# Stack loads in SyncE's queue, stores a cycle later, and maxima split before their transpose, in a fused attention and Fourier-mixing kernel

## Chip, cores and metric

One Trainium2 chip, one of its cores. The metric is the device time of one execution in microseconds (us), as the median over several runs. A second figure, the span, comes from one profiled execution and goes from its first to its last instruction.

## The reference

Two blocks read the same `x` of 2048 rows by 640 columns, and a gate mixes them row by row. All is float32.

```python
def _A_ref(x, wqkv, wo):                 # attention: H = 32 heads of Dh = 20
    qkv = (x @ wqkv).reshape(B, S, 3, H, Dh)   # then q, k, v by head
    scores = einsum("bhqd,bhkd->bhqk", q, k) * Dh ** -0.5
    p = softmax(scores, axis=-1)
    o = einsum("bhqk,bhkd->bhqd", p, v)
    return o.reshape(B, S, D) @ wo
def _B_ref(x, seq_re, seq_im, hid_re, hid_im):   # real part of a 2-D DFT
    a = einsum("bsd,ed->bse", x, hid_re)
    b = einsum("bsd,ed->bse", x, hid_im)
    return einsum("ts,bse->bte", seq_re, a) - einsum("ts,bse->bte", seq_im, b)
g = sigmoid((x * gate_w).sum(-1, keepdims=True))
return g * _A_ref(x, wqkv, wo) + (1 - g) * _B_ref(x, ...)
```

## The kernel before

Products that need more than one pass of TensorE's rounded float32 are written as three products of a value split into a rounded part and a remainder (`split`, `three`). q, k and v are projected first; q and k go in two parts to `qk_scr` in device memory, v to `v_scr`.

Attention works by units: 32 units, each of two heads and half of the 2048 queries; two units that share their heads are a pair. For a pair, `load_stack` brings k's parts into one of two `kst` buffers and q's parts into one of two `qst` buffers by 12 DMAs (four for k, four for each half of the queries): 40 rows from both parts at once, and 20 rows from the first part. A unit has 32 steps. Each step `e` computes, for two heads, a 128x512 block of transposed scores (L685) and its exponential on ScalarE (L687). The maximum that the softmax subtracts is computed ahead by a second pass over the scores (`m`, L159) and a reduction on VectorE (L161); this pass runs LEAD = 41 steps ahead. When a unit's maxima are complete, `max_nm` reduces them to 128x16 with the sign turned, `max_chain` transposes that on TensorE (L193), splits the result into `m1` and `m2`, and four DMAs write the rows into `qst`, where they act as two more rows of the contraction. `av_step` (L448) multiplies probabilities with v and a column of ones, which gives the sum of each row.

After a unit, `unit_end` copies the accumulator to `o` (ScalarE) and lists its follow-ups by steps: store the row sums (`store_l`), load them spread over partitions (`load_l`), reciprocal on VectorE (`recip`), store and broadcast it (`store_r`, `load_r`), multiply `o` on GpSimd (`norm`) and store it (`store_o`).

The Fourier block fills TensorE's room in the same loop. `hid_tile` makes the hidden-dimension products (stored to `a_scr`), and from about 640 us on `dft_step` does the sequence dimension in 56 units of 16 steps: `load_c` brings DFT matrices (`in_cdft`), `load_a` the operand (`araw`), both added and split on GpSimd; results are summed over several units through `y_scr` (`yt` is an earlier sum loaded again, `finish_y` adds and stores).

The order is written out by hand. One cycle is four steps of attention, and the string gives the order of TensorE's instructions in it: `e` and `m` one score matmul each, `F` a share of the fill, `B` the burst of 16 `av` matmuls, with the maxima's reduction ahead of them and their transpose behind. All DMAs and off-path work are listed with `at_step(i, fn)` and issued when step `i` begins:

```python
ORDER = "emFemFFFFemFeFFmeFFemFFFmmFFmeeB"
def burst(c):
    for n in ends:
        max_nm(n)
    run_extras(max(done - HIDS, 0) // 3, 2)
    for kt in (2 * c, 2 * c + 1):
        av_step(now[0], kt // NS, kt % NS)
    while ends:
        max_chain(ends.pop(0))
```

SyncE (SP) carries nearly all DMAs in one queue, in the order of the steps; an instruction that waits holds those behind it. GpSimd (POOL) carries the stack's DMAs among its additions and splits. At the end, `rest` holds the follow-ups of the last unit, and the output product runs tile by tile.

Of the kernel before, what the change touches and what calls it, by code (L numbers as in the profile page):

```python
# [10 lines left out]
F32 = mybir.dt.float32  # L11
R = mybir.dt.float32r
AF = mybir.ActivationFunctionType
ALU = mybir.AluOpType
AX = mybir.AxisListType
# [3 lines left out]
P = 128  # L19
# [7 lines left out]
HE = D // 2  # L27
VW = 2 * (DH + 1)
KROWS = 3 * DH
NU = 2 * NP  # L30
# [25 lines left out]
UNITS = len(PRODUCTS) * HT  # L56


def f32(ap):
    return ap.bitcast(F32)  # L60
# [3 lines left out]
def mix_kernel(ctx: ExitStack, tc: tile.TileContext, xa, wqk, wb, cdft, wo, out):  # L64
# [8 lines left out]
    small = pools(name="small", bufs=1)  # L73
# [24 lines left out]
    def split(dst1, dst2, src, e1, e2):  # L98
        if e1 is act:
            act.activation(dst1, src, AF.Copy)  # L100
        else:
            e1.tensor_copy(dst1, src)  # L102
        e2.tensor_tensor(dst2, src, f32(dst1), op=ALU.subtract)  # L103
# [8 lines left out]
    def bank():  # L112
        return ps_w.tile([P, 512], F32, name=f"ps{next(turn) % 5}")
# [13 lines left out]
    def load_stack(p):  # L127
        kt, qt = kst[p % 2], qst[p % 2]
        u = S // 2
        for t, o, two, one, cs in ((kt, D, 0, 2, slice(0, S)), (qt, 0, 1, 0, slice(0, u)), (qt, 0, 1, 0, slice(u, S))):  # L130
            for h in range(2):
                r = (2 * p + h) * DH
                b = 64 * h
                rows = slice(o + r, o + r + DH)
                yield f32(t[b + two * DH : b + (two + 2) * DH, cs]), qk_scr[:, rows, cs]
                yield f32(t[b + one * DH : b + (one + 1) * DH, cs]), qk_scr[0, rows, cs]
# [8 lines left out]
    def at_step(i, fn):  # L145
        later.setdefault(i, []).append(fn)
# [24 lines left out]
            max_chain(n - 1)  # L171

    def max_nm(n):
        nms[n] = small.tile([P, 16], F32, name="nm", bufs=2)
        dve.tensor_reduce(nms[n], mx.pop(n).rearrange("p h q c -> p (h q) c"), axis=AX.X, op=ALU.max, negate=True)

    def s_step(i):
        for fn in [s_mm(i, h) for h in range(2)]:
# [10 lines left out]

    def max_chain(n):  # L190
        q = q_unit(n)
        pt = bank()[:16, :P]
        pe.transpose(pt, nms.pop(n), ident)  # L193
        m1 = small.tile([16, P], R, name="m1", bufs=2)
        m2 = small.tile([16, P], R, name="m2", bufs=2)
        split(m1, m2, pt, dve, dve)

        def rows():
            for h in range(2):
                b = 64 * h + KROWS  # L200
                sp.dma_start(f32(q[b : b + 1, :]), f32(m1[8 * h : 8 * h + 8, :]))
                sp.dma_start(f32(q[b + 1 : b + 2, :]), f32(m2[8 * h : 8 * h + 8, :]))

        if now[0] < 0:
            rows()
        else:
            at_step(now[0] + 2, rows)


    pa = pools(name="att", bufs=1)  # L210
# [195 lines left out]
    def load_c(g):  # L406
        n, j = divmod(g, 2)
        n, t = divmod(n, HT)
        raws = []
        for i, (_, th, ri) in enumerate(PRODUCTS[n][0]):  # L410
            raw = apool[0].tile([P, 1024], F32, name="raw2", bufs=2) if i and apool else raw_tile()
            o = (2 * ri + j) * 1024
            sp.dma_start(raw, cdft[th * HT + t, :, o : o + 1024])
            raws.append(raw)

        def finish():
            c = cparts[g] = part_tile()
            if len(raws) > 1:
                pool.tensor_tensor(raws[0], raws[0], raws[1], op=ALU.add if PRODUCTS[n][0][1][0] > 0 else ALU.subtract)  # L419
            split(c[:, 0], c[:, 1], raws[0], pool, pool)  # L420

        return finish
# [28 lines left out]
            unit_end(i, n)  # L451

    def unit_end(i, n):
        o = pa.tile([P, 512], F32, name="o")
        act.activation(o, av, AF.Copy)
        lc = pa.tile([P, 16], F32, name="lc")
        rb = pa.tile([P, 512], F32, name="rb")

        q = pool if n == NU - 1 else sp

        def store_l():
            q.dma_start(l_scr[n], o.rearrange("(j r) c -> j r c", j=4)[:, DH])

        def load_l():
            q.dma_start(lc, l_scr[n].rearrange("j (a b) -> (j a) b", b=16))

        def recip():
            dve.reciprocal(lc, lc)

        def store_r():  # L470
            q.dma_start(r_scr[n].rearrange("j (a b) -> (j a) b", b=16), lc)

        def load_r():
            for j in range(4):
                q.dma_start(rb[32 * j : 32 * j + 32, :], r_scr[n, j : j + 1].to_broadcast([32, 512]))

        def norm():
            pool.tensor_tensor(o, o, rb, op=ALU.mult)  # L478

        def store_o():  # L480
            for qc in range(2):
                for h in range(2):
                    j = 2 * qc + h
                    t0 = (n % 2) * (S // 2) + qc * 512
                    r = (2 * (n // 2) + h) * DH
                    q.dma_start(o_scr[r : r + DH, t0 : t0 + 512], o[32 * j : 32 * j + DH, :])

        steps = (1, 4, 10, 12, 15, 23, 25) if n < NU - 2 else (1, 4, 10, 12, 15, 19, 21)
        for k, fn in zip(steps, (store_l, load_l, recip, store_r, load_r, norm, store_o)):
            if n == NU - 1:  # L490
                rest.append(fn)
            else:
                at_step(i + k, fn)
# [7 lines left out]
    def dft_step(g):  # L501
        n, t, s = g // NS // HT, g // NS % HT, g % NS
        if s == 0:
            new_y(0), new_y(1)
            outs[n, t] = []
            for _, th, hf in PRODUCTS[n][2]:
                tt = th * HT + t
                y = None
                if (tt, hf) in signs:
                    y = apool[0].tile([P, HE], F32, name="yt", bufs=4)  # L510
                    sp.dma_start(y, y_scr[tt, :, hf * HE : (hf + 1) * HE])
                outs[n, t].append(y)
        if s % 8 == 0 and g // 8 + 3 < 2 * UNITS:
            cfin.append(load_c(g // 8 + 3))
        if s % 8 == 4 and cfin and g // 8 + 2 < 2 * UNITS:
            cfin.pop(0)()
        c = cparts[g // 8]
        cs = slice((s % 8) * P, (s % 8 + 1) * P)
        a = at[n % 2, s]
        for z, (cz, az) in enumerate(((0, 0), (0, 1), (1, 0))):  # L520
            for h in range(2):
                r = slice(64 * h, 64 * h + 64)
                pe.matmul(yp[h][:, :HE], c[r, cz, cs], a[r, az], start=s == 0 and z == 0, stop=s == NS - 1 and z == 2)  # L523
            if z < 2:
                yield
        w = g % (HT * NS) - 16
        if n + 1 == len(PRODUCTS) and w >= 0:
            d, r = divmod(w, 8)
            if r == 0 and d < ND:
                wos[d] = raw_tile()[:, :D]  # L530
                sp.dma_start(wos[d], wo[:, d])
            if r == 5 and d < ND:
                raw = wos.pop(d)
                for h in range(2):
                    wos[d, h] = a_tile(1, 2 * d + h)
                    split(wos[d, h][:, 0], wos[d, h][:, 1], raw[:, h * HE : (h + 1) * HE], pool, pool)
        if s == NS - 1:
            m = apool[0].tile([P, HE], F32, name="m", bufs=2)
            y0, y1 = yp[0][:, :HE], yp[1][:, :HE]

            def read():
                act.activation(m, y0, AF.Copy)
                dve.tensor_tensor(m, y1, m, op=ALU.add)  # L543

            extras.append((now[0], read))
            for out_, y in zip(PRODUCTS[n][2], outs.pop((n, t))):
                extras.append((now[0] + 5, functools.partial(finish_y, out_, t, m, y)))
        yield

    def finish_y(target, t, m, y):  # L550
        sg, th, hf = target
        tt = th * HT + t
        if (tt, hf) in signs:
            pool.tensor_tensor(y, y, m, op=ALU.add if sg == signs[tt, hf] else ALU.subtract)  # L554
        else:
            signs[tt, hf] = sg
            y = m
        at_step(now[0] + 4, functools.partial(sp.dma_start, y_scr[tt, :, hf * HE : (hf + 1) * HE], y))

    preps = []  # L560

# [69 lines left out]
    def begin(i):  # L631
        now[0] = i
        n, s = divmod(i, 32)
        for fn in later.pop(i, ()):
            fn()
        if s % 2 == 0:
            flush()
        if s == 0 and n % 2 == 0:
            p = n // 2
            if p + 1 < NP:  # L640
                at_step(i + 6, functools.partial(load_v, p + 1))
                for j, args in enumerate(load_stack(p + 1)):
                    at_step(i + 2 + 2 * j, functools.partial(pool.dma_start, *args))
        if i < total:
            pts[n, s // 2, s % 2] = pair_tile()

# [145 lines left out]
```

## Time and profile before

| | |
|---|---|
| median of 3 runs | 1954.19 us (1954.18 to 1955.42) |
| profiled execution | 1953.52 us |
| its span | 1951.7 us |
| granted TensorE clock, mean | 0.997 |
| busy: TensorE, VectorE, ScalarE, GpSimd | 98%, 75%, 62%, 54% of the span |
| DMA | 281 MB, 144 GB/s on average |
| DMAs of the stack, all from GpSimd | 192 |

The loop over attention and Fourier work lasts from 279 us to 1873 us: 256 cycles, of about 6.2 us in the hidden-dimension part and 6.1 to 6.3 us in the part of the DFT. Ahead of it lie the projections, behind it the output product. In the rows of the profile, `L161` is a line of the kernel, `PEld` is TensorE's weight load, a name ending in `q` is the queue of an engine, and what stands in brackets is idle time ahead of the first instruction and what ended it.

### The profile page before, as it was taken

The numbers are of one execution on the slowest core, as the hardware profiler recorded it, in microseconds if no ns is written. First come the engines' busy times: TensorE is split into PE (matmuls) and PEld (weight loads), VectorE is DVE, ScalarE is ACT, GpSimd is POOL, SyncE is SP. The second block draws the span as 40 slices with busy tenths as digits, with TensorE's granted clock in tenths as the row PEclk, the third lists the DMA queues.
The fourth block names the chain that finished last, engine by engine and source line by source line (L and its number), as shares of the span: only waits on it lengthen the run. The fifth ranks groups of instructions, "written<-read, shape, count | busy, mean of one in ns | idle before, by whom it ended". The sixth has DMA issues, their size and how long they took to land. (4 is left out here: it accounts for less than half of the span.)

```text
span 1951.7 us, 43695 instructions
## 1 busy us (share of the span) xinstructions
PE 1918.5 (98%) x17080; PEld 1375.4 (70%) x17080; DVE 1454.1 (75%) x2419; ACT 1211.8 (62%) x2337; POOL 1045.8 (54%) x975
## 2 busy tenths in 40 slices
PE   8999999999999999999999999999999999999999
PEld 7987767777775667666666666666666666666679
DVE  4144568889887888888888878888888887888323
ACT  4221147777776676666776766676766776776741
POOL 1210001111005989457469968995786789787512
PEclk9999999999999999999999999999999999999999
DMA  7763321212114584435356746664554565454355
GB/s 224 173 172 127 130 100 46 78 61 74 47 58 141 170 228 152 122 116 149 97 173 199 196 154 189 212 177 123 149 171 125 183 169 181 154 149 147 98 165 179
DMA packets 196414, 281.02 MB, mean 144 GB/s; under 512 B 73272, under 2 KB 137816, under 8 KB 194288
## 3 DMA queue, kind: packets, MB, share of 16 engines
q1 hardware_dynamic: 158992, 246.20, 40.8%
q0 software_dynamic: 37216, 32.03, 6.7%
q8 instruction: 134, 2.20, 0.5%
q14 instruction: 72, 0.59, 0.1%
HBM read 213.81 MB, written 63.70 MB: 142 GB/s over the span
## 5 line engine op out<-in xcount | busy, mean ns | idle before, releaser
L161 DVE TENSOR_REDUCE mx<-ps 128x1 f32<-128x512 f32 x2048 | 1287.4, 683 | 197.4 <-PE ps L159 178.8
L687 ACT ACTIVATE p<-ps 128x512 f32<-128x512 f32 x2048 | 1080.9, 598 | 443.4 <-PE ps L159 241.2
L159 PE MATMUL ps<-kst,qst 60*128 60x512 f32 x2048 | 776.1, 427 | 8.0 <-DVE mx L161 3.2
L685 PE MATMUL ps<-qst,kst 62*128 62x512 f32 x2048 | 700.7, 422 | 5.8 <-DMA qst<-m 4.2
L523 PE MATMUL yp<-a,part 64*128 64x320 f32 x5376 | 687.6, 309 | 0.1
L523 PEld LDWEIGHTS yp<-a,part 64*128 64x128 f32 x5376 | 593.7, 186 | 15.3 <-DVE m L543 0.3
L448 PE MATMUL av<-p,v 128*21 128x512 f32 x4096 | 494.4, 599 | 0.1
L685 PEld LDWEIGHTS ps<-qst,kst 62*128 62x128 f32 x2048 | 335.5, 185 | 215.2 <-DVE mx L161 181.9
L159 PEld LDWEIGHTS ps<-kst,qst 60*128 60x128 f32 x2048 | 364.5, 185 | 38.2 <-DVE mx L161 11.8
L103 POOL TENSOR_TENSOR part<-raw,part 128x1024 fp32r<-128x1024 f32 x112 | 267.2, 2386 | 9.0
L448 PEld LDWEIGHTS av<-p,v 128*21 128x21 f32 x4096 | 98.3, 100 | 226.8 <-issue 223.1
L301 PE MATMUL yp<-wb,xs 64*128 64x320 f32 x1920 | 237.4, 309 | 3.7 <-ACT raw L309 3.5
L301 PEld LDWEIGHTS yp<-wb,xs 64*128 64x128 f32 x1920 | 206.8, 187 | 8.9 <-ACT raw L309 4.1
L419 POOL TENSOR_TENSOR raw<-raw,raw 128x1024 f32<-128x1024 f32 x78 | 187.4, 2402 | 17.3 <-DMA raw<-in_cdft 11.8
L102 POOL CAST part<-raw 128x1024 fp32r<-128x1024 f32 x112 | 116.4, 1039 | 116.8 <-PE yp L523 87.4
L102 POOL CAST wb<-raw 128x966 fp32r<-128x966 f32 (+1 forms) x4 | 3.4, 856 | 215.8 <-PE ps L159 215.8
L554 POOL TENSOR_TENSOR yt<-yt,m 128x320 f32<-128x320 f32 x64 | 55.5, 878 | 111.3 <-DVE m L543 104.2
L478 POOL TENSOR_TENSOR o<-o,rb 128x512 f32<-128x512 f32 x32 | 41.4, 1294 | 134.5 <-DMA rb<-r_scr 73.7
L103 POOL TENSOR_TENSOR a<-araw,a 128x320 fp32r<-128x320 f32 x112 | 97.8, 873 | 9.0
L103 DVE TENSOR_TENSOR p<-ps,p 128x512 fp32r<-128x512 f32 x40 | 27.5, 691 | 94.1 <-ACT p L100 91.4
L106 PE MATMUL ps<-xs,part 128*128 128x512 f32 x200 | 80.2, 401 | 7.8 <-ACT xs L100 6.1
L100 ACT ACTIVATE p<-ps 128x512 fp32r<-128x512 f32 x40 | 23.7, 597 | 101.4 <-PE ps L108 101.4
(67 smaller groups left out, 1331.8 us busy)
## 6 DMA issues: line engine op xcount, KB each, us to landing
raw<-in_cdft SPq DMA_DIRECT2D x192, 512.0 KB
araw<-a_scr SPq DMA_DIRECT2D x192, 160.0 KB
qk_scr<-p SPq DMA_DIRECT2D x40, 512.0 KB
kst<-qk_scr POOLq DMA_DIRECT2D x32, 320.0 KB, 12.3
qst<-qk_scr POOLq DMA_DIRECT2D x64, 160.0 KB, 8.2
a_scr<-raw SPq DMA_DIRECT2D x64, 160.0 KB
yt<-y_scr SPq DMA_DIRECT2D x64, 160.0 KB
y_scr<-yt SPq DMA_DIRECT2D x64, 160.0 KB
```

Of the source, the lines that this page charges most:

```text
L102: e1.tensor_copy(dst1, src)
L103: e2.tensor_tensor(dst2, src, f32(dst1), op=ALU.subtract)
L106: pe.matmul(ps, st1, mv1, start=first, stop=False)
L159: pe.matmul(ps, q[b : b + KROWS, qt * P : (qt + 1) * P], k[b : b + KROWS, kc * 512 : (kc + 1) * 512], start=True, stop=True)
L161: return lambda: dve.tensor_reduce(mx[n][:, h, qt, kc : kc + 1], ps, axis=AX.X, op=ALU.max)
L301: pe.matmul(yp[h][:, :HE], xs[r, xz, d, cs], w[r, wz, d, :HE], start=d == 0 and z == 0, stop=d == ND - 1 and z == 2)
L419: pool.tensor_tensor(raws[0], raws[0], raws[1], op=ALU.add if PRODUCTS[n][0][1][0] > 0 else ALU.subtract)
L448: pe.matmul(av[32 * j : 32 * j + DH + 1, :], v[:, kt, h * (DH + 1) : (h + 1) * (DH + 1)], pp[qc][:, h, :], start=kt == 0, stop=kt == NS - 1)
L523: pe.matmul(yp[h][:, :HE], c[r, cz, cs], a[r, az], start=s == 0 and z == 0, stop=s == NS - 1 and z == 2)
L554: pool.tensor_tensor(y, y, m, op=ALU.add if sg == signs[tt, hf] else ALU.subtract)
L685: pe.matmul(pt, k[b : b + KROWS + 2, kt * P : (kt + 1) * P], q[b : b + KROWS + 2, qc * 512 : (qc + 1) * 512], start=True, stop=True)
L687: act.activation(pts[n, kt, qc][:, h], pt, AF.Exp, scale=float(DH) ** -0.5)
```

## The change

Three parts, all within the main loop's lists. First, `load_stack`'s DMAs for the next pair go from GpSimd's queue to SP's, at other steps (before: every second step from 2 to 24). Second, follow-ups of a unit come later, `o` has two buffers, stores to `y_scr` are listed 8 instead of 4 steps behind the finish, and `yt` is loaded in the middle of a DFT unit, after that unit's `in_cdft` load. Third, the maxima are split into two parts on VectorE before they are transposed; the transpose then has 32 instead of 16 columns of weights, one copy takes its result out of PSUM, and one DMA for each head writes two rows.

```diff
     def max_nm(n):
-        nms[n] = small.tile([P, 16], F32, name="nm", bufs=2)
-        dve.tensor_reduce(nms[n], mx.pop(n).rearrange("p h q c -> p (h q) c"), axis=AX.X, op=ALU.max, negate=True)
+        nm = small.tile([P, 2, 8], F32, name="nm", bufs=2)
+        dve.tensor_reduce(nm, mx.pop(n), axis=AX.X, op=ALU.max, negate=True)
+        nms[n] = small.tile([P, 2, 2, 8], R, name="nms", bufs=2)
+        split(nms[n][:, :, 0], nms[n][:, :, 1], nm, dve, dve)
...
     def max_chain(n):
-        pt = bank()[:16, :P]
-        pe.transpose(pt, nms.pop(n), ident)
-        m1 = small.tile([16, P], R, name="m1", bufs=2)
-        m2 = small.tile([16, P], R, name="m2", bufs=2)
-        split(m1, m2, pt, dve, dve)
+        pt = bank()[:32, :P]
+        pe.transpose(pt, f32(nms.pop(n)).rearrange("p h z q -> p (h z q)"), ident)
+        m = small.tile([32, P], F32, name="m")
+        dve.tensor_copy(m, pt)
         def rows():
             for h in range(2):
                 b = 64 * h + KROWS
-                sp.dma_start(f32(q[b : b + 1, :]), f32(m1[8 * h : 8 * h + 8, :]))
-                sp.dma_start(f32(q[b + 1 : b + 2, :]), f32(m2[8 * h : 8 * h + 8, :]))
+                sp.dma_start(f32(q[b : b + 2, :]), m[16 * h : 16 * h + 16, :])
...
-            at_step(now[0] + 2, rows)
+            at_step(now[0] + 3, rows)
...
     def unit_end(i, n):
-        o = pa.tile([P, 512], F32, name="o")
+        o = pa.tile([P, 512], F32, name="o", bufs=2)
...
-        steps = (1, 4, 10, 12, 15, 23, 25) if n < NU - 2 else (1, 4, 10, 12, 15, 19, 21)
+        steps = (6, 10, 16, 23, 27, 34, 45) if n < NU - 2 else (1, 4, 10, 12, 15, 19, 21)
         for k, fn in zip(steps, (store_l, load_l, recip, store_r, load_r, norm, store_o)):
...
     def dft_step(g):
         if s == 0:
             new_y(0), new_y(1)
             outs[n, t] = []
+        if s % 8 == 0 and g // 8 + 3 < 2 * UNITS:
+            cfin.append(load_c(g // 8 + 3))
+        if s % 8 == 4 and cfin and g // 8 + 2 < 2 * UNITS:
+            cfin.pop(0)()
+        if s == 8:
             for _, th, hf in PRODUCTS[n][2]:
                 ...
                     sp.dma_start(y, y_scr[tt, :, hf * HE : (hf + 1) * HE])
-        if s % 8 == 0 and g // 8 + 3 < 2 * UNITS:
-            cfin.append(load_c(g // 8 + 3))
-        if s % 8 == 4 and cfin and g // 8 + 2 < 2 * UNITS:
-            cfin.pop(0)()
...
     def finish_y(target, t, m, y):
-        at_step(now[0] + 4, functools.partial(sp.dma_start, y_scr[tt, :, hf * HE : (hf + 1) * HE], y))
+        at_step(now[0] + 8, functools.partial(sp.dma_start, y_scr[tt, :, hf * HE : (hf + 1) * HE], y))
...
     def begin(i):
-                for j, args in enumerate(load_stack(p + 1)):
-                    at_step(i + 2 + 2 * j, functools.partial(pool.dma_start, *args))
+                for j, args in zip((4, 6, 8, 10, 11, 12, 13, 14, 34, 37, 40, 43), load_stack(p + 1)):
+                    at_step(i + j, functools.partial(sp.dma_start, *args))
```

## The prediction

> **What bounds the kernel now.** I read the page first, its busy rows above all.
>
> ```profile
> span 1951.7 us, 43695 instructions
> PE 1918.5 (98%) x17080; PEld 1375.4 (70%) x17080; DVE 1454.1 (75%) x2419; ACT 1211.8 (62%) x2337; POOL 1045.8 (54%) x975
> ```
>
> TensorE is busy for 98% of the span. All that scheduling can win is the 33 us in which it is not, and what a stall does to the matmuls after it. So the next view is the list of TensorE's waits (line, releaser, us in total, times, longest).
>
> ```profile
> PE ps L685 <- DMA qst<-m: 4.2, 2, 3.3
> PE yp L301 <- ACT raw L309: 3.5, 2, 2.7
> PE ps L159 <- DVE mx L161: 3.2, 4, 1.2
> PE ps L159 <- DMA qst<-qk_scr: 2.4, 1, 2.4
> ```
>
> Few and short: two waits for the rows of maxima, one for the stack, two for the hidden product's read. Their true price shows in the timeline of TensorE. One cycle of ORDER begins where the `av` matmuls of the last one's burst begin, so the distance of two such rows is a cycle.
>
> ```profile
> 1000.11 1.92 PE L448 MATMUL av<-p,v 128*21 128x512 f32 x16
> 1006.19 1.92 PE L448 MATMUL av<-p,v 128*21 128x512 f32 x16
> ...
> 1124.88 1.91 PE L448 MATMUL av<-p,v 128*21 128x512 f32 x16
> 1133.93 0.89 PE L685 MATMUL ps<-qst,kst 62*128 62x512 f32 x2 [3.28 <-DMA qst<-m]
> 1134.75 3.01 PE L448 MATMUL av<-p,v 128*21 128x512 f32 x16
> 1142.02 1.49 PE L448 MATMUL av<-p,v 128*21 128x512 f32 x12
> ...
> 1615.00 1.91 PE L448 MATMUL av<-p,v 128*21 128x512 f32 x16
> 1622.04 0.76 PE L159 MATMUL ps<-kst,qst 60*128 60x512 f32 x1 [2.40 <-DMA qst<-qk_scr]
> 1638.59 1.91 PE L448 MATMUL av<-p,v 128*21 128x512 f32 x16
> ```
>
> An undisturbed cycle takes 6.08 us (6.1 in the following); divided by its four steps that is 1.52 us a step. The two cycles from 1124.88 take 17.14 us where 12.2 are due: 4.9 lost to a wait of 3.28. The three from 1615.00 take 23.59 where 18.5 are due (18.3, and 0.2 for a transpose): 5.1 lost. The excess over the wait is the clock:
>
> ```profile
> 1130.00:1140.00 10.00, 6.72 (x49) 3.38 (x48) 4.04 (x7) 3.63 (x8) 9.71 (x6) 0.83 0.25 92
> ```
>
> In 1130 to 1140 the granted clock was 0.83 (third number from the end), and the same 16 `av` matmuls that took 1.92 us took 3.01.
>
> Why were the rows late at 1134? SP's and POOL's timelines:
>
> ```profile
> 1114.39 0.38 SPq L635 DMA_DIRECT2D y_scr<-m  x1
> 1124.67 1.42 SPq L486 DMA_DIRECT2D o_scr<-o  x4
> 1127.83 0.68 SPq L201 DMA_DIRECT2D qst<-m  x1
> 1131.39 0.63 SPq L202 DMA_DIRECT2D qst<-m  x1
> ...
> 1123.34 1.30 POOL L478 TENSOR_TENSOR o<-o,rb 128x512 f32<-128x512 f32 x1
> ```
>
> SP issues nothing from 1114.8 to 1124.67: the head of its queue is the store of `o`, which waits for POOL's multiply `norm` (1123.34) and POOL comes to it no earlier. The rows of maxima stood behind that store. Over the whole run SP's longest sums of waiting behind the projection are of this kind:
>
> ```profile
> SPq L462 <- ACT p L687: 166.8, 29, 9.2
> SPq L471 <- DVE lc L468: 149.5, 28, 10.4
> SPq L486 <- POOL o L478: 108.0, 25, 14.9
> ```
>
> **The stores, a cycle later.** `store_l` goes from step 1 to 6 after a unit's end, `store_o` from 25 to 45 with `norm` from 23 to 34, the stores to `y_scr` from 4 to 8 steps. Each then stands in SP's queue some 4 to 11 steps behind what it stores, 6 to 17 us at 1.52 us a step, so most of the 424 us in the three rows above stops blocking. `o` gets a second buffer, which the 45 steps (more than a unit's 32) need; there is no new wait on ACT. The rows of maxima, now 3 instead of 2 steps behind the burst, no longer have `store_o` ahead of them (it falls 13 steps into the next unit). The extra step costs 1.5 us; two DMAs instead of four save two issues of 0.63 to 0.68, about 1.3. Net nothing, and the first score that needs the rows comes five steps, 7.6 us, behind them. So the loss at 1134 goes: **-4.9** (bounds -4.9 and 0). What is late next is no other transfer: the 6.1 us cycles around show none waiting.
>
> **The stack, from POOL's queue to SP's.**
>
> ```profile
> L635 POOL DMA_DIRECT2D qst<-qk_scr x120 | 69.4, 586 | 25.7 <-DMA kst<-qk_scr 25.6
> L635 POOL DMA_DIRECT2D kst<-qk_scr x60 | 34.8, 585 | 73.3 <-PE ps L159 73.2
> qst<-qk_scr POOLq DMA_DIRECT2D x64, 160.0 KB, 8.2
> ```
>
> 180 issues leave POOL: 104 us of work and 99 of waiting. POOL is off the path; what this buys is that `norm` and the splits are on time. On SP an issue costs what its rows above show, 0.3 to 0.7 us, so 12 per pair of units are 4 to 8 us of 97, beside idle time. The Trainium skill (DMA: Bandwidth & Descriptors, section "Issuing engines are not separate DMA queues") says that such a move saves only issue time, since all queues share the same DMA engines; by it the landing times stay as they are.
>
> Deadline: LEAD puts the first maximum that needs the new stack about 24 steps into the pair, 36.5 us. Its last load is now nominally 14 steps in, 21.3 us; with the median of 8.2 it lands at 29.5. Before, the nominal place was step 16, but POOL was behind, and at 1622 the load came 2.4 us late. That term goes, with the second wait for rows at 1638: **-5.1** (bounds -5.1, and a loss that is priced as the first rival).
>
> **Hidden product to DFT.** At 593 to 617 ACT's read waits for a `raw` buffer that a late `in_cdft` load holds:
>
> ```profile
> 593.38 1.92 PE L448 MATMUL av<-p,v 128*21 128x512 f32 x16
> 601.18 1.92 PE L448 MATMUL av<-p,v 128*21 128x512 f32 x16
> 607.43 1.91 PE L448 MATMUL av<-p,v 128*21 128x512 f32 x16
> 612.42 0.93 PE L301 MATMUL yp<-wb,xs 64*128 64x320 f32 x2 [2.65 <-ACT raw L309]
> 617.07 1.49 PE L448 MATMUL av<-p,v 128*21 128x512 f32 x12
> ```
>
> Beside 6.25 undisturbed, 7.80 and 9.64: 1.6 and 3.4 lost. The first `in_cdft` pair now has four `kst` loads ahead of it in one queue, the second has the `qst` loads before it instead of beside it. I take 0 for the first (bounds -1.6 and +4) and half for the second, **-1.7** (bounds -3.4 and +2).
>
> **Maxima split ahead of the transpose.** VectorE's chain was reduce, transpose, two reads of PSUM. It becomes reduce, copy, subtract, transpose, one read. The nearest rows for the two new operations on 128x16:
>
> ```profile
> L102 DVE CAST m<-ps 16x128 fp32r<-16x128 f32 x32 | 8.9, 279 | 17.9 <-PE ps L193 17.5
> L103 DVE TENSOR_TENSOR m<-ps,m 16x128 fp32r<-16x128 f32 x32 | 8.9, 278 | 1.1
> L392 DVE TENSOR_SCALAR ngate<-gate 128x16 f32<-128x16 f32 x1 | 0.2, 175 | 0.0
> ```
>
> Between 175 (the same shape and a plain operation, which I take) and 278. A read of 279 goes. VectorE gains or loses 0.1 us a unit; what matters is that the transpose, in TensorE's queue ahead of all scores of the next cycle, comes 0.35 to 0.56 us later by this chain. Is there room?
>
> ```profile
> 1119.73 0.21 DVE L175 TENSOR_REDUCE nm<-mx 128x16 f32<-128x64 f32 x1
> 1120.41 0.09 PEld L193 LDWEIGHTS ps<-ident,nm 128*16 128x16 f32 x1 [0.85 <-DVE nm L175]
> ...
> 1001.95 0.18 PEld L685 LDWEIGHTS ps<-qst,kst 62*128 62x128 f32 x1 [0.85 <-DVE mx L161]
> ```
>
> The view blames VectorE for 0.85 us, but `nm` had ended at 1119.94, 0.47 before, and a cycle without a transpose has the same 0.85: it is the change from `av` to the next shape. So 0.47 us are covered. Two operations of 0.175 and some 0.05 of gaps fit; at 0.278 each 0.15 would stick out. Over 31 units: 0 to +4.7; I take **+1.0**, since the cover is nearly used up. The transpose itself streams 128 columns as before.
>
> **The loads of yt** move half a DFT unit later, behind the `in_cdft` load. A DFT unit lasts 3.5 cycles, 14 steps, so they are still about 7 steps and the 5 of the finish ahead of their use, 18 us. Nothing, unless SP is a cycle late.
>
> **Sum.** -4.9 - 5.1 - 1.7 + 1.0 = -10.7. The profiled execution took 1953.5 us (1.8 beyond its span), 0.7 below the median of the runs, 1954.2. So 1942.8 for such an execution, 1943.5 as a median; I say 1943. With all terms at their good ends (-4.9 - 5.1 - 1.6 - 3.4) -15.0: 1939. The longest of the waits for `mx` in the list, 1.2, may go as well, if VectorE no longer stands at the reciprocal of `lc` there: with it, and as a profiled execution, 1937. Bad ends without the rivals, half of the first two terms (+5.0) and +3.7 at the transpose: 1952.
>
> **Rivals.** First, slower: *the stack late behind SP's own queue*. All of it now stands in order behind `load_l`, v, the splits' loads and one another, and four loads of `kst` issued at once take 13.5 us and more, where one 20-row load of `qst` took 2.5:
>
> ```profile
> DMA to landing us min/median/max: 13.5/13.7/13.8
> DMA to landing us min/median/max: 2.5/2.5/2.5
> ```
>
> So the loads queue among themselves. If SP is one cycle late at step 14 (6.1 us) and a load takes 11, it lands at 38.4 against 36.5: 1.9 us of TensorE in each of 15 loads, +28, and 1943 + 28 = 1971; it decides from 7 us of lateness (36.5 - 29.5). For it: the 10 us in which SP stood at 1114. Against: what made SP stand is just what is moved. The Trainium skill (the same page, section "Why a DMA increments its semaphore by 16 and not by 1") speaks for it: the number of engines of a transfer divides the slowest dimension of both sides, which for the 40-row loads with a source of 2 by 20 rows leaves two engines, and on SP's queue always the lowest. No row here names an engine, so no run shown can tell. Chance 0.24.
>
> Second, about the same: *the transpose sticks out and the gain is half*. With the split at its dear end (+4.7 instead of +1.0) and SP still standing where `norm` is late, so that only the stack's term is won: 1954.2 - 5.1 + 4.7 = 1954. For it: cover of 0.47 against 0.45 needed; against: the plain operation's 175 ns. Chance 0.13.
>
> **How the numbers follow.** Forecast 0.63, rivals 0.24 and 0.13. The measurement can tell about 0.2% (3.9 us) from no change. Faster: the forecast and a little of the second, 0.64; same 0.13; slower 0.23. The forecast's own range is 1937 to 1952; to leave no more than 0.2 outside, the range reaches into the weak half of the first rival (a late stack in every second pair, +14 on 1943, and a little): 1937 to 1960.
>
> **What would show it.** Right: no wait of TensorE for `qst<-m` or `qst<-qk_scr`, every cycle after 640 us at 6.1 to 6.5 us, SP's waits for ACT, `lc` and `o` nearly gone, POOL without DMA issues between 300 and 1800 us, the weight load of the transpose still 0.85 us after its predecessor. Wrong: waits of L159 for the stack at pair starts, VectorE waiting for `lc`, a wait above 0.9 us at L193, or a granted clock below 1 at new places.

## Result and profile after: slower by 2.3%

The changed kernel takes 2001.4 us (median of 5 runs), the kernel before beside it 1955.4: a ratio of 1.0234, 95% interval [1.0216, 1.0252]. The forecast was 1943, in a range of 1937 to 1960. The profiled execution has a span of 1997.4 us. The page's busy rows:

```profile
span 1997.4 us, 43597 instructions
PE 1928.4 (97%) x17080; PEld 1382.3 (69%) x17080; DVE 1488.8 (75%) x2451; ACT 1211.8 (61%) x2337; POOL 943.5 (47%) x795
```

TensorE has the same 17080 matmuls, and GpSimd is 102 us lighter, as forecast. VectorE is 35 us heavier with 32 instructions more, which is over 1 us for each of them. The list of TensorE's waits answers the one shown of before:

```profile
PE ps L195 <- DVE nms L103: 20.8, 15, 3.7
PE ps L159 <- DMA qst<-qk_scr: 8.6, 2, 5.2
PE yp L301 <- ACT raw L309: 7.6, 1, 7.6
...
PE ps L159 <- DMA y_scr<-yt: 5.6, 1, 5.6
PE ps L159 <- DMA araw<-a_scr: 3.8, 1, 3.8
```

The waits for `qst<-m` are gone. Two kinds have come: the transpose (now L195) waits for the split, 15 times, and the maxima (L159) for the stack. L159 reads only `kst` and `qst`, so the two waits put down to `y_scr` and `araw` are the stack's as well. The timeline of TensorE at one of these, in the ninth pair:

```profile
1133.62 1.92 PE L448 MATMUL av<-p,v 128*21 128x512 f32 x16
1143.63 0.76 PE L159 MATMUL ps<-kst,qst 60*128 60x512 f32 x1 [5.20 <-DMA qst<-qk_scr]
1146.81 2.51 PE L448 MATMUL av<-p,v 128*21 128x512 f32 x16
1149.63 0.28 PE L195 MATMUL ps<-ident,nms 128*32 128x128 f32 x1 [0.31 <-DVE nms L103]
1154.10 1.92 PE L448 MATMUL av<-p,v 128*21 128x512 f32 x16
```

The two cycles from 1133.62 take 20.5 us in place of 12.4 (two of 6.08, and 0.28 for the transpose). Behind the stall the granted clock (third number from the end) was 0.50, and `av` took 2.51 us in place of 1.92:

```profile
1143.60:1147.00 3.40, 3.37 (x22) 2.85 (x26) 2.43 (x4) 0.12 (x1) 3.25 (x3) 0.50 0.92 290
```

SP's timeline ahead of it, where the pair began at 1102.2 (its first score on TensorE):

```profile
1101.29 0.63 SPq L636 DMA_DIRECT2D kst<-qk_scr  x1
...
1105.58 0.36 SPq L636 DMA_DIRECT2D kst<-qk_scr  x1
1113.57 0.57 SPq L462 DMA_DIRECT2D l_scr<-o  x1
1114.19 0.65 SPq L636 DMA_DIRECT2D kst<-qk_scr  x1
...
1119.58 7.12 SPq L636 DMA_DIRECT2D qst<-qk_scr  x2
...
1132.26 0.60 SPq L636 DMA_DIRECT2D qst<-qk_scr  x1
...
1133.84 0.36 SPq L636 DMA_DIRECT2D qst<-qk_scr  x1
```

SP issues nothing from 1105.9 to 1113.6, and stands again after 1120 and before 1132. The last load of the first half of the queries goes out 31.6 us after the pair's start, in place of the nominal 21.3; TensorE needs it at 36.2 and has it at 41.4. SP's own waits say for what it stood:

```profile
SPq L636 <- DMA kst<-qk_scr: 58.9, 18, 7.4
SPq L486 <- DMA kst<-qk_scr: 30.0, 8, 6.0
SPq L413 <- DMA qst<-qk_scr: 25.2, 11, 4.2
```

A store of `o` (L486) or a load from `in_cdft` (L413) has nothing to do with a stack load. In the records of the trace SP's 1352 DMAs use eight completion semaphores in turn, 169 each, and a DMA is issued only when the one eight places ahead of it has landed (all its data have arrived and its semaphore says so). The store of row sums at 1113.57 is eight places behind the 40-row load of 1101.29, so it went out only when that load had landed, 12 us after its issue. Before, GpSimd's stack loads had eight other semaphores.

And the split, in the timelines of VectorE, GpSimd and TensorE:

```profile
1360.84 0.21 DVE L175 TENSOR_REDUCE nm<-mx 128x16 f32<-128x64 f32 x1
1360.86 2.35 POOL L103 TENSOR_TENSOR part<-raw,part 128x1024 fp32r<-128x1024 f32 x1
1361.08 2.16 DVE L102 CAST nms<-nm 128x16 fp32r<-128x16 f32 x1
1363.28 0.18 DVE L103 TENSOR_TENSOR nms<-nm,nms 128x16 fp32r<-128x16 f32 x1
...
1363.51 0.28 PE L195 MATMUL ps<-ident,nms 128*32 128x128 f32 x1 [1.92 <-DVE nms L103]
```

The copy of 16 numbers a partition takes 2.16 us: it ends 0.03 us after GpSimd's subtraction, which began 0.22 ahead of it. The subtract behind it, with GpSimd idle, takes 0.18. Over the whole run every copy or subtract of this kind that took more than 0.2 us ended 0.03 to 0.04 us after an instruction of GpSimd that had begun before it. In the view of the tile (duration in ns, least, median, most):

```profile
L102 DVE CAST nms<-nm x32: 174/176/2160, 222.3 to 1870.6; 128x16 fp32r<-128x16 f32 x32
L103 DVE TENSOR_TENSOR nms<-nm,nms x32: 174/176/2264, 222.5 to 1870.8; 128x16 fp32r<-128x16 f32 x32
```

In the first eight units, up to 625 us, while GpSimd is idle beside them, every one takes 0.174 to 0.177.

### The profile page after: what moved, and what is told of

Its sections match the earlier page's. It is cut to its first block, busy times and chain, and to the rows that moved or that the text cites. A ratio compares the mean times of both kernels' runs of the same rounds, so it can differ in the third digit from the quotient of the medians.

```text
span 1997.4 us, 43597 instructions
## 1 busy us (share of the span) xinstructions
PE 1928.4 (97%) x17080; PEld 1382.3 (69%) x17080; DVE 1488.8 (75%) x2451; ACT 1211.8 (61%) x2337; POOL 943.5 (47%) x795
## 4 chain that ended last, share of the span: by engine, by line
PE 79%; DMA 10%; DVE 6%; issue 2%; POOL 1%; ACT 1%; SPq 1%; POOLq 0%; ACTq 0%; DVEq 0%
PE av L448 19%; PE yp L524 16%; PE ps L686 15%; PE ps L159 11%; PE yp L301 6%; DVE mx L161 4%; PE ps L106 4%; PE ps L108 4%; PE ps L107 4%; DMA kst<-qk_scr 4%; DMA qst<-qk_scr 3%; DMA raw<-in_xa 1%; DVE nms L102 1%; DMA y_scr<-m 1%; DVE nms L103 1%
## 5 line engine op out<-in xcount | busy, mean ns | idle before, releaser
L159 PE MATMUL ps<-kst,qst 60*128 60x512 f32 x2048 | 778.8, 428 | 22.5 <-DMA qst<-qk_scr 8.6
L159 PEld LDWEIGHTS ps<-kst,qst 60*128 60x128 f32 x2048 | 367.2, 186 | 50.3 <-issue 23.1
L478 POOL TENSOR_TENSOR o<-o,rb 128x512 f32<-128x512 f32 x32 | 41.4, 1292 | 188.5 <-DMA rb<-r_scr 188.5
```

The lines of the kernel that those rows point to most:

```text
L159: pe.matmul(ps, q[b : b + KROWS, qt * P : (qt + 1) * P], k[b : b + KROWS, kc * 512 : (kc + 1) * 512], start=True, stop=True)
```

## Experiments

All kernels are the changed one or the one before with the edits shown; the ratio is against the kernel before on the same chip, whose medians there were 1957.6 to 1958.8.

**Third part undone in the changed kernel.**

```diff
     def max_nm(n):
...
-        nms[n] = small.tile([P, 2, 2, 8], R, name="nms", bufs=2)
-        split(nms[n][:, :, 0], nms[n][:, :, 1], nm, dve, dve)
...
     def max_chain(n):
...
+        pe.transpose(pt, nms.pop(n), ident)
...
+        split(m1, m2, pt, dve, dve)
...
-            at_step(now[0] + 3, rows)
+            at_step(now[0] + 2, rows)
```

> The changed kernel with its third part undone: maxima transposed first and split afterwards, four DMAs, as before. In the changed kernel's trace the cycles with a transpose lose 27 us more than before (33.9 against 5.0 us of excess, and 1.9 of it elsewhere), and VectorE's copy and subtract of 128x16 take up to 2.26 us where 0.175 is the least; each long one ends when GpSimd's instruction beside it ends. Theory: these two operations are that cost. Expected 2001 - 27 = 1974, cycles with a transpose at 6.3 to 6.5 us again, and the stack's late landings still there. Rival (the stack in SP's queue is the whole cost and the waits at the transpose only take up time that would be lost anyway): 1995 or more.

It took 1987.7 us, ratio 1.0151 [1.0116, 1.0186]: 14 us won (16 by the ratios), not 27. The waits at the transpose are gone, but those of L159 for the stack rise from 18.0 to 23.9 us:

```profile
PE ps L159 <- DMA qst<-qk_scr: 17.7, 4, 5.5
...
PE ps L159 <- DMA raw<-in_cdft: 6.2, 1, 6.2
```

Neither theory had the number. That a stall at the transpose gives the loads time does not explain it: in the next run those stalls are gone as well, and the stack's waits stay at 18.4 us. What this run has more than the next one is four DMAs for the rows of each unit in SP's queue in place of two. The last load of a first half went out 28.5 us into the pair on average, against 27.6 both in the changed kernel and in the next run. That the two more DMAs are the reason is argued from this, not shown by a run of its own.

**Reduced maxima in PSUM.**

```diff
-        nm = small.tile([P, 2, 8], F32, name="nm", bufs=2)
+        pt = bank() if now[0] >= 0 else None
+        nm = small.tile([P, 2, 8], F32, name="nm") if pt is None else pt[:, P : P + 16].rearrange("p (h q) -> p h q", h=2)
...
```

> The changed kernel, but the reduced maxima are written into the PSUM bank that the transpose will use anyway, so that copy and subtract read PSUM and not two operands in SBUF; same number of instructions in the same order (the first unit, ahead of the loop, stays in SBUF). Theory (the two operations stand while GpSimd works, because both sides of the copy and both inputs of the subtract lie in SBUF): both take 0.15 to 0.25 us every time, the transpose waits at most 0.1 us, and the time is that of the kernel with the part undone, 1974, within 4 us. Rival (the chain is merely two operations longer, or VectorE is held by something else): the waits at the transpose stay and the time is 1995 to 2001.

It took 1976.0 us, ratio 1.0086 [1.0062, 1.0111], within what was expected. The instructions and their order are the same; only the reduced maxima lie elsewhere:

```profile
L102 DVE CAST nms<-ps x31: 173/174/175, 315.5 to 1850.5; 128x16 fp32r<-128x16 f32 x31
L103 DVE TENSOR_TENSOR nms<-ps,nms x31: 173/174/175, 315.7 to 1850.7; 128x16 fp32r<-128x16 f32 x31
```

All 62 take 0.173 to 0.175 us, beside a GpSimd as busy as in the changed kernel (943.8 and 943.5 us). The rival (a chain two operations longer) falls.

**Stack back in GpSimd's queue.**

```diff
-                for j, args in zip((4, 6, 8, 10, 11, 12, 13, 14, 34, 37, 40, 43), load_stack(p + 1)):
-                    at_step(i + j, functools.partial(sp.dma_start, *args))
+                for j, args in enumerate(load_stack(p + 1)):
+                    at_step(i + 2 + 2 * j, functools.partial(pool.dma_start, *args))
```

> The changed kernel with the stack's DMAs back in GpSimd's queue at every second step from 2 to 24, as before. Theory (a 40-row load takes some 12 us to land, SP's eight completion semaphores go round, so SP stands until the load eight DMAs ahead has landed, and the last loads of the stack are issued at 30 to 35 us where they are needed at 36): the waits at pair starts (4.6, 6.9, 6.9 and 4.7 us of excess) go, with 3 to 4 us of half clock behind them, and part of the 10 us lost at 616: expected 1970 to 1976, with the waits at the transpose still there. Rival (the transposes are the whole cost): 1995 or more.

It took 1965.0 us, ratio 1.0031 [1.0015, 1.0046], even below what was expected. No wait of TensorE for a load is left in the loop; those at the transpose stay:

```profile
PE ps L195 <- DVE nms L103: 21.6, 17, 3.7
PE ps L106 <- ACT xs L100: 6.1, 1, 6.1
PE ps L106 <- ACT v L280: 2.2, 1, 2.2
PE ps L159 <- DVE mx L161: 1.7, 2, 0.8
```

**40-row loads cut in two, on SP.**

```diff
-                yield f32(t[b + two * DH : b + (two + 2) * DH, cs]), qk_scr[:, rows, cs]
+                yield [(f32(t[b + (two + z) * DH : b + (two + z + 1) * DH, cs]), qk_scr[z, rows, cs]) for z in range(2)]
...
```

> The changed kernel with each 40-row load of the stack cut into two of 20 rows, at the same steps in SP's queue: 18 DMAs for a pair instead of 12, the same bytes. Theory (what holds SP is the landing of the 40-row loads, which move as if on two DMA engines, where a 20-row load landed 2.5 us after its issue): SP's waits for kst and qst loads fall from over 200 us to under 60, no wait of TensorE for the stack, and as in the run with the stack on GpSimd 1970 to 1976. Rival (what makes SP late is the number of DMAs and their order in one queue): six more DMAs for a pair, slower than 2001 by some 5 us or no better.

It took 1961.6 us, ratio 1.0020 [1.0007, 1.0032]: more DMAs in the same queue, and 40 us less. SP's waits for stack loads fell from 229.5 us in total to 19.7; the three largest sums are:

```profile
SPq L637 <- DMA kst<-qk_scr: 7.7, 13, 1.2
SPq L487 <- DMA kst<-qk_scr: 7.2, 12, 1.0
SPq L429 <- DMA kst<-qk_scr: 2.2, 3, 0.9
```

So what holds SP is not the number of DMAs but how long one takes to land; the last load of a first half now goes out 18.4 us into the pair on average (27.6 in the changed kernel). The trace's packets show why: of the 40-row load issued at 376.6 us in the changed kernel, the 40 packets of 8 KB run two at a time, 0.31 us each, for some 7 us; of the same rows as two loads, issued at 373.8 in this kernel, ten and more run at a time, and all 40 have ended 3.3 us after the first issue.

**The later stores alone.** Stack and maxima as before.

> The stores a cycle later and yt in the middle of its unit, alone: the stack back in GpSimd's queue and the maxima transposed first, both as before. In the run with the stack on GpSimd all cycles but those with a transpose lost 8.7 us against 24.9 before. Theory (the third part of the change is the only loss left there, and the later stores do what was forecast of them): about 16 us less than before, 1938 to 1942. Rival (the gain of the later stores needs the stack out of GpSimd's queue, because GpSimd is late to the multiply of o): 1950 to 1957.

It took 1940.9 us, ratio 0.9898 [0.9877, 0.9920], as the theory had it. What is left of the loop's waits for loads is the one for the stack on GpSimd, as before:

```profile
PE ps L159 <- DMA qst<-qk_scr: 2.4, 1, 2.4
```

**Both repairs.** The changed kernel with cut loads and the maxima in PSUM.

> The changed kernel with both repairs: the stack's 40-row loads cut in two on SP's queue, and the reduced maxima in PSUM. Theory (two separate costs, 27 us at the transposes and the rest at SP's queue, which add up): 1961.6 - 25.5 = 1936, faster than before by 1.0%. Rival (taking away the waits at the transposes lets the next wait come in, since the stalls gave the loads time): 1945 or more.

It took 1936.3 us, ratio 0.9881 [0.9861, 0.9902]: the two repairs add up as the theory had it, and the rival falls.

**Cut loads, third part undone.**

> The changed kernel with the stack's loads cut in two on SP's queue and the third part undone (transpose first, split from PSUM afterwards, four DMAs). Theory (split ahead of the transpose has no gain of its own where it costs no wait): the same time as with both repairs, 1936, within 3 us. Rival (two DMAs instead of four for the rows, or the shorter hold of VectorE behind the transpose, are worth something): 1939 to 1945.

It took 1935.8 us, ratio 0.9871 [0.9850, 0.9891]: the best of all, together with the one above. The third part has no gain of its own. Whether SP's queue is a better place for cut loads than GpSimd's was not run beside the later stores. TensorE's longest waits:

```profile
PE ps L106 <- ACT xs L100: 6.2, 1, 6.2
PE ps L159 <- DVE mx L161: 1.7, 2, 0.8
PE ps L106 <- ACT part L100: 1.3, 1, 1.3
PE ps L688 <- DVE mx L161: 1.1, 1, 1.1
```

Once the projections have begun TensorE waits for no load any more, and never above 1.3 us.

**The third part alone, on the kernel before.**

> The kernel before with the third part of the change alone: maxima split ahead of their transpose, two DMAs, one step later. Theory (copy and subtract wait for GpSimd's instruction whatever else is in the queues): 20 to 27 us more than before, 1977 to 1984, nearly all of it in cycles with a transpose. Rival (the waits come of the order that the other two parts give GpSimd): below 1965.

It took 1987.5 us, ratio 1.0138 [1.0109, 1.0166], at the upper edge of what was expected or beyond it. The mechanism needs nothing of the other parts:

```profile
PE ps L195 <- DVE nms L103: 25.0, 17, 3.3
```

**The same with the maxima in PSUM.**

> The kernel before with the third part alone, the reduced maxima in PSUM instead of SBUF. The part alone with them in SBUF measured 1987. Theory (the wait for GpSimd is all that it costs): 1954 to 1960, copy and subtract at 0.174 us in all units of the loop, no wait of TensorE above 0.2 us at the transpose. Rival (the split ahead of the transpose costs by its length): 1965 or more.

It took 1957.9 us, ratio 1.0001 [0.9985, 1.0017]: nothing is left of the cost.

**The stack in SP's queue alone, on the kernel before.**

> The kernel before with the stack's 12 DMAs in SP's queue at the change's steps; stores and maxima as before. Theory (a 40-row load holds SP for its landing of 12 us through the eight completion semaphores): slower than before, 1965 to 1990, with waits of TensorE for the stack and for the rows of maxima at pair starts. Rival (the stack on SP hurts only beside the later stores): 1950 to 1958.

It took 2020.1 us, ratio 1.0312 [1.0294, 1.0329], more than the whole change and more than expected; the expected waits for the rows of maxima did not come:

```profile
PE ps L159 <- DMA qst<-qk_scr: 43.2, 9, 7.7
```

Beside the early stores SP stands both for landings (254 us for stack loads) and for ScalarE and GpSimd (164 for the row sums, L462, and 56 for `o`, L486). In the changed kernel, with the later stores, these are 230, 71 and 9 us; with stack and stores but without the third part the time was 1987.7.

**Cut loads on GpSimd, in the kernel before.**

> The kernel before, with the stack's 40-row loads cut in two 20-row loads in GpSimd's queue, at the same steps; nothing else. Theory (the landing of the 40-row loads is what makes the stack slow in either queue, but before only one stack load was late, and SP does not stand for GpSimd's loads): landings of kst fall from a median of 12.3 us to under 6, the wait at 1622 goes or stays by GpSimd's own lateness, 1948 to 1956, no more than 0.4% faster. Rival (the loads' landings held SP's transfers too, through the shared DMA engines): the wait for the rows at 1134 goes as well, 1944 or less.

It took 1952.6 us, ratio 0.9970 [0.9959, 0.9981]. The landings are more than halved. These are the rows of the DMA issues (KB each and median us), first of the kernel before, then of this run:

```profile
kst<-qk_scr POOLq DMA_DIRECT2D x32, 320.0 KB, 12.3
kst<-qk_scr POOLq DMA_DIRECT2D x32, 160.0 KB, 12.3
```

```profile
kst<-qk_scr POOLq DMA_DIRECT2D x96, 160.0 KB, 5.3
```

TensorE's wait for the stack is gone, and those for the rows stay:

```profile
PE ps L687 <- DMA qst<-m: 7.4, 2, 4.5
```

## Why the prediction was wrong, step by step

**Later stores, -4.9.** Right in mechanism, too small. With the part alone the loss at 1134 went, and also the two losses from 593 to 617 and one at the reciprocal of `lc`; at these places every cycle is now within 0.5 us of an undisturbed one. The part is worth -1.0%, some 18 us.

**Hidden product to DFT, -1.7.** The forecast looked for this term in the stack's place among the loads. The later stores alone take these losses away, with the stack where it was. With the stack on SP the place became worse, not better: one wait of 7.6 us in place of two of 3.5 together, in a cycle of 16.6 us, where 5.0 were lost before and 10.3 now.

**Stack to SP, -5.1.** The step that failed is the sum "last load nominally 14 steps in, 21.3 us, with the median of 8.2 it lands at 29.5". It counted SP's issues (4 to 8 us a pair, which is right) and not that a queue with eight completion semaphores stands for the landing of the DMA eight ahead; that such a move changes only issue time did not come true. In the ninth pair the last load went out at 31.6 us and was there at 41.4. That is the first rival, with its place (L159 at pair starts) but a larger price: 28 us were named, and the stack back on GpSimd is worth 1.0234 - 1.0031, 2.0% or 40 us. It had 0.24. The evidence lay in a row that the prediction quoted: on GpSimd too the `qst` loads had stood 25.6 us for the landing of `kst` loads. Its comparison of 13.5 us with 2.5 did not tell the sizes apart: two of the four `kst` loads have 20 rows, and behind the 40-row loads they landed as late. The Trainium skill's rule on the number of engines (DMA: Bandwidth & Descriptors, section "Why a DMA increments its semaphore by 16 and not by 1") was cited for that rival; the packets, two at a time for 40 rows, agree with it. So do the two last updates of the semaphore of the 40-row load of 1101.29, at 1113.34 and 1113.51 us. The argument against the rival, that what made SP stand is moved away, overlooked that the moved loads bring their own reason to stand.

**Split ahead of the transpose, +1.0.** The cover was read rightly: with both operations at 0.174 us the transpose waits for nothing, and the part costs nothing (1.0001). The failed term is the duration, taken from a row of 0.175 us for the same shape, which ran once, when GpSimd had no work. Beside GpSimd it was up to 2.26 us, and the part alone costs 1.4%, some 27 us. The dear end of the range (0.278, a read of PSUM) was no bound: PSUM reads are the ones that do not wait. The Trainium skill states it (SBUF — State Buffer, section "Who interferes with whom"): a VectorE copy in its two-port mode, or an operation with two inputs in SBUF, contends with a GpSimd instruction that reads SBUF, and the one issued second blocks until the first has finished. The trace agrees: the long ones ended 0.03 to 0.04 us after GpSimd's instruction; no run shows the copy's mode. The prediction did not weigh this rule, and gave the effect no rival of that size.

**The sum.** Forecast -10.7. Measured apart: -1.0% for the stores, +3.1% for the stack, +1.4% for the split; together +2.3%. The split costs about the same in three places: 1.4% alone, 1.5% in the changed kernel (1.0234 against 1.0086) and 1.4% beside cut loads (1.0020 against 0.9881). What does not add up is stores and stack: the later stores lessen what the stack does. The signs named for "wrong" came all but one: waits of L159 at pair starts, more than 0.9 us at the transpose, a granted clock below 1 at new places; only VectorE's wait for `lc` did not grow (9.1 us, 10.3 before).

## What to carry to other kernels

Before a DMA is moved to another queue, ask how long it takes to land and how many that queue can have in flight: a slow one holds every DMA behind it, and cutting it along its source's slowest dimension was worth as much here as putting it back in the other queue (1961.6 and 1965.0 us). Before an operation is put on VectorE beside a busy GpSimd, look where its operands lie; a duration from a time when GpSimd is idle is no price. Where a change has parts, cost each against the resource that it newly shares, not only against the one that it relieves.

## What the runs showed of the hardware

- In the changed kernel a VectorE copy of 128x16 from SBUF to SBUF took 0.174 us alone and up to 2.16 us beside GpSimd; the subtract with both inputs in SBUF up to 2.26; with the source in PSUM both took 0.173 to 0.175 in all 31 units of the loop.
- A load of 40 rows from a source of 2 by 20 rows moved two packets of 8 KB at a time, some 7 us for all 40, and the same rows as two loads ten and more, 3.3 us from the first issue to the end; in the changed kernel cutting these loads was worth 2001 against 1962 us.
- Two cycles with a stall of TensorE of 5.2 us took 8.0 more than undisturbed ones: behind it the granted clock was 0.50 for 3.4 us, and the `av` matmuls ran for 2.51 us in place of 1.92 (0.3 are a wait at the transpose).
